# Low halves moved to VectorE and the exponents' clamp to GpSimd in the first block, one more unit scored in plain float32

## The chip, the cores and the metric

One NeuronCore of one Trainium2 chip. The metric is the device time of one execution in microseconds. Five engines run their own instruction queues in order: TensorE (PE, matrix products, with its weight loads shown as PEld), VectorE (DVE), ScalarE (ACT), GpSimd (POOL) and SyncE (SP), which issues all DMA transfers here. An engine waits for another through semaphores only.

## The reference

Three stages, in float32:

- Retention: for each of 4 x 8 heads a state of 64 x 64 decays by gamma at each of 768 positions and takes up the outer product of k and v; the output is q times the state. 
- A feed-forward layer on 3072 tokens: `h = x @ w_in` (512 to 2048), an ELU, `@ w_out` (2048 to 512).
- A second one: `h = x @ w_in` (512 to 1024), h times its softmax, a layer norm with gain `g_ln`, `@ w_out` (1024 to 512).

q, k and v come as float32; the weights of both layers are passed on as the bits of float64.

## The kernel before

Precision: a product of two float32 matrices is made of three passes in a rounded format, float32r. Each operand is split into a high half (the rounded copy) and a low half (the operand minus its high half); `mm3` multiplies high by high, high by low and low by high (L65 to L67).

Weights: a piece is [128, 512] in float64. `load_w` (L93) loads it, `abs_w` (L98, ScalarE) takes the absolute value of the upper word, `bits_w` (L103, VectorE) builds the float32 bits in four operations: clamp of the exponent (L107), first logical operation (L110), shift (L112), second logical operation (L114). A call works on two pieces, the first and third operation on one and the second and fourth on the piece before, alternating. `split_w` (L116) rounds the high half on ScalarE (L124) and subtracts the low half on GpSimd (L125). `prep_w` (L128) is one slot of this pipeline: split of piece n - 2, abs of n + 1, bits of n and n - 1, load of n + 3. Pieces stand in pools of four buffers.

Retention runs in chunks of 128 positions. A unit is a chunk's two head pairs. `att_scores_u` (L176) scores a whole unit in plain float32 and masks it on VectorE (L184); `att_scores` (L188) scores a pair from the split parts that `split_unit` (L165) makes on ScalarE and GpSimd (L170 to L173). Units below `UN` (17) go the first way. `att_values` (L205) makes the output of a pair (L225) and updates the state (L230, L233).

Order: the program is written out in the order of issue, without a scheduler. The start (L384 to L423) does eight units of retention and four slots of the weights' pipeline. The block loop (L426 to L507) has six blocks of 512 tokens with 16 steps each. A step s multiplies into the hidden layer (`ff1_in`), takes the ELU (`elu_a`, `elu_b`), handles one pair of retention for the block after, and multiplies out of the hidden layer for step s - 2 (`ff1_out`). In block 0 a step also holds two slots of `prep_w`. `elu_b` combines on VectorE (L276 in block 0), rounds the high half gh on ScalarE (L280), and subtracts the low half gl on GpSimd (L281). At a block's last step `split_xh` (L238, ScalarE) and `split_xl` (L244, VectorE) split the next block's input; it has one buffer. In the last block a step holds one slot of `prep_w` for the second layer's weights. A third loop (L511 to L526) does the second layer, 24 tiles of 128 tokens.

The functions and the lines that call them:

Of the kernel before, what the change touches and what calls it, by code (L numbers as in the profile page):

```python
# [9 lines left out]
F32 = mybir.dt.float32  # L10
F32R = mybir.dt.float32r
U32 = mybir.dt.uint32
AF = mybir.ActivationFunctionType
ALU = mybir.AluOpType
# [4 lines left out]
P = 128  # L19
B, H, S, D = 4, 8, 768, 64  # L20
NT = B * S
DM = H * D
FF1, FF2 = 2048, 1024
NP = H // 2          # head pairs; a pair fills 128 partitions
NCH = S // P         # chunks of a sequence
TB = 512             # tokens of a block of the first feed-forward layer
NB = NT // TB
CPB = TB // P
NF1 = FF1 // P
NF2 = FF2 // P  # L30
KD = DM // P
NU = B * NCH * 2      # a unit is a chunk's two head pairs
PPB = CPB * NP       # head pairs of a block
LAG = 2              # steps from a product into the hidden layer to the one out of it
HL = NF1 - 2         # step at which the weights are ready and the split of q and k begins
PRE = (2, 3, 4, 5)    # units of the start behind which a slot of the weights' pipeline lies
LEAD = 2             # pairs by which the attention is ahead of its block
UN = PPB + LEAD // 2  # units before this one score in plain float32
E_MIN, E_MAX = (float(x) for x in np.array([896 << 20, 1151 << 20], np.uint32).view(np.float32))
GAMMA = [1.0 - 2.0 ** (-5.0 - h) for h in range(H)]  # L40

# [2 lines left out]
def tile_retention_ffn(ctx, tc, k_t, qk_dup, qkv, w_in1, w_out1, w_in2, w_out2, g_ln, dmask, odec, kdec, ident_in, out):  # L44
    nc = tc.nc
# [4 lines left out]
    wa_p = ctx.enter_context(tc.tile_pool(name="wa", bufs=32))  # L50
# [10 lines left out]
    y_dr = [dram.tile([CPB, P, KD, P], F32, name=f"y_dr{i}") for i in range(NB)]  # L61

    def mm3(o, lh, ll, rh, rl, first, last):
        """o += (lh + ll).T @ (rh + rl) in float32r passes."""
        nc.tensor.matmul(o, lh, rh, start=first, stop=False)  # L65
        nc.tensor.matmul(o, lh, rl, start=False, stop=False)  # L66
        nc.tensor.matmul(o, ll, rh, start=False, stop=last)  # L67

    with tc.manual_schedule():
# [7 lines left out]
        wb_p = ph1.enter_context(tc.tile_pool(name="wb", bufs=32))  # L77
# [6 lines left out]
        stage_p = ph0.enter_context(tc.tile_pool(name="stage", bufs=4, side="right"))  # L84
        kblk = [at_p.tile([P, 2, 2, P], F32, name=f"kblk{i}", bufs=1) for i in range(2)]

# [1 line left out]
        # They come as float64, whose bits are cut to float32's here: a piece is [128, 512].  # L88
        raw_t, abs_t, w1i, w1o, w2i, w2o = {}, {}, {}, {}, {}, {}
        srcs = {"w1i": w_in1, "w1o": w_out1, "w2i": w_in2, "w2o": w_out2}  # L90
        dsts = {"w1i": w1i, "w1o": w1o, "w2i": w2i, "w2o": w2o}
# [3 lines left out]
            nc.sync.dma_start(out=t.rearrange("p a b -> p (a b)"), in_=srcs[x[0]][x[1]].bitcast(U32))  # L95
            raw_t[x] = t

        def abs_w(x):  # L98
            a = stage_p.tile([P, 512], U32, tag="wt", name="wt")
            nc.scalar.activation(a.bitcast(F32), raw_t[x][:, :, 1].bitcast(F32), AF.Abs)  # L100
            abs_t[x] = a

        def bits_w(x, y):  # L103
            """The first two operations on piece x and the last two on piece y."""
            if x:
                a = abs_t[x]
                nc.vector.tensor_scalar(a.bitcast(F32), a.bitcast(F32), E_MAX, E_MIN, ALU.min, ALU.max)  # L107
            if y:
                t, b = raw_t.pop(y), abs_t[y]
                nc.vector.scalar_tensor_tensor(b, t[:, :, 1], 0xC0000000, b, ALU.bitwise_and, ALU.bitwise_or)  # L110
            if x:
                nc.vector.tensor_scalar(a, a, 3, 0x3FFFFFF8, ALU.logical_shift_left, ALU.bitwise_and)  # L112
            if y:
                nc.vector.scalar_tensor_tensor(b, t[:, :, 0], 29, b, ALU.logical_shift_right, ALU.bitwise_or)  # L114

        def split_w(x):  # L116
            name, f = x
            w = abs_t.pop(x).bitcast(F32)
            if name == "w2o":
                nc.vector.tensor_scalar(w, w, g_sb[:, f:f + 1], None, ALU.mult)  # L120
            pool, tag = (wb_p, "wb") if name == "w1o" else (wa_p, "wa")
            hi = pool.tile([P, 512], F32R, tag=tag, name=f"{name}h")
            lo = pool.tile([P, 512], F32R, tag=tag, name=f"{name}l")
            nc.scalar.copy(hi, w)  # L124
            nc.gpsimd.tensor_tensor(lo, w, hi.bitcast(F32), ALU.subtract)  # L125
            dsts[name][f] = (hi, lo)

        def prep_w(order, n):  # L128
            """One slot of the weights' pipeline."""
            at = lambda i: order[i] if 0 <= i < len(order) else None  # L130
            if at(n - 2):
                split_w(at(n - 2))
            if at(n + 1):
                abs_w(at(n + 1))
            bits_w(at(n), at(n - 1))
            if at(n + 3):
                load_w(at(n + 3))

# [2 lines left out]
            order1 += [x for x in (("w1o", f), ("w1i", f + 3)) if x[1] < NF1]  # L141
        order2 = [("w2i", j) for j in range(2 * KD)] + [("w2o", j) for j in range(NF2)]

# [1 line left out]
        qk_t, in_t, hl_t, p_t = {}, {}, {}, {}  # L145

        def load_unit(u):
# [15 lines left out]
            nc.gpsimd.tensor_tensor(kt, kt, kd_sb[:, h:h + 4].unsqueeze(2).to_broadcast([P, 4, D]), ALU.mult)  # L163

        def split_unit(u):  # L165
            """q's and k's parts: q's high one twice over and its low one, k's high one over its low one."""
            t = qk_t.pop(u)
            q2 = hl_p.tile([P, 4, 2, P], F32R, tag="q2", name="q2")
            k2 = hl_p.tile([P, 4, P], F32R, tag="k2", name="k2")
            nc.scalar.copy(k2, t[:, 1])  # L170
            nc.scalar.copy(q2[:, :, 0, :], t[:, 0])
            nc.gpsimd.tensor_tensor(k2[D:], t[D:, 1], k2.bitcast(F32)[D:], ALU.subtract)
            nc.gpsimd.tensor_tensor(q2[:, :, 1, :], t[:, 0], q2.bitcast(F32)[:, :, 0, :], ALU.subtract)  # L173
            hl_t[u] = (q2, k2)

        def att_scores_u(u, bank):  # L176
            """A unit's scores in plain float32."""
            h = 4 * (u % 2)
            pt = at_p.tile([P, 4, P], F32, tag="pt", name="pt")
            sc = bank.rearrange("p (h t) -> p h t", h=4)  # L180
            for i in range(2):
                for j in range(2):
                    nc.tensor.matmul(sc[:, 2 * i + j, :], kblk[u % 2][:, i, j, :], in_t[u][:, i * P:(i + 1) * P], start=True, stop=True)
            nc.vector.tensor_tensor(pt, sc, dm_sb[:, h:h + 4, :], ALU.mult)  # L184
            for i in range(2):
                p_t[2 * u + i] = pt[:, 2 * i:2 * i + 2, :]

        def att_scores(n, bank):  # L188
            """A pair's scores from the split parts."""
            u, i = divmod(n, 2)  # L190
            h = 4 * (u % 2) + 2 * i
            pt = at_p.tile([P, 2, P], F32, tag="pt", name="pt")
            q2, k2 = hl_t[u]
            sc = bank.rearrange("p (j a t) -> p j a t", j=2, a=2)
            for j in range(2):
                nc.tensor.matmul(sc[:, j].rearrange("p a t -> p (a t)"), k2[:, 2 * i + j, :], q2[:, 2 * i + j].rearrange("p a t -> p (a t)"), start=True, stop=True)
            sa = hl_p.tile([P, 2, P], F32, tag="sa", name="sa")
            nc.scalar.copy(sa, sc[:, :, 1, :])  # L198
            nc.vector.tensor_tensor(pt, sa, sc[:, :, 0, :], ALU.add)  # L199
            nc.vector.tensor_tensor(pt, pt, dm_sb[:, h:h + 2, :], ALU.mult)  # L200
            if i:
                del hl_t[u]
            p_t[n] = pt
# [42 lines left out]
            for cc in cs:  # L246
                engines[cc % len(engines)].tensor_tensor(xl[:, cc], xf[:, cc], xh.bitcast(F32)[:, cc], ALU.subtract)  # L247

# [1 line left out]
        h_t, g_t, acc_t = {}, {}, {}  # L250

        def ff1_in(s):
# [18 lines left out]
        def elu_b(s, on_act):  # L271
            e = g_t[s]
            gh = g_p.tile([P, TB], F32R, tag="gh", name="gh")
            gl = g_p.tile([P, TB], F32R, tag="gl", name="gl")
            if on_act:
                nc.vector.scalar_tensor_tensor(e, e, -1.0, h_t.pop(s), ALU.add, ALU.max)  # L276
            else:
                nc.vector.tensor_scalar(e, e, 1.0, -1.0, ALU.min, ALU.add)  # L278
                nc.vector.tensor_tensor(e, e, h_t.pop(s), ALU.max)  # L279
            nc.scalar.copy(gh, e)  # L280
            nc.gpsimd.tensor_tensor(gl, e, gh.bitcast(F32), ALU.subtract)  # L281
            g_t[s] = (gh, gl)

        def new_acc(tb):
# [19 lines left out]
                    nc.sync.dma_start(out=y_dr[tb][:, :, m, :].rearrange("c p t -> p c t"), in_=yt.rearrange("p (c t) -> p c t", c=CPB))  # L304
                del acc_t[tb]

# [1 line left out]
        N2 = NT // P  # L308
        yin, ysp, h2, zc_t, rs_t, zt_t, op_t = {}, {}, {}, {}, {}, {}, {}

# [70 lines left out]
                nc.sync.dma_start(out=out[i * P:(i + 1) * P, :], in_=ot)  # L381
                del zt_t[i], op_t[i]

# [1 line left out]
        nc.vector.memset(state, 0.0)  # L385
        for kb in kblk:
            for j in range(2):
# [12 lines left out]
        load_unit(2)  # L400
        scale_k(0)
        slot = -1
        XLE = (nc.vector,)
        UB = PPB // 2
        for u in range(UB):
            if u + 1 < UB:
# [15 lines left out]
                prep_w(order1, slot)  # L422
                slot += 1  # L423

# [1 line left out]
        NS = NB * NF1  # L426
        NPR = B * NCH * NP
        for s in range(NS + LAG):
# [35 lines left out]
            if tb == 0:  # L464
                prep_w(order1, slot)
                slot += 1
            if s == HL:
                for i in range(slot, len(order1) + 2):
                    prep_w(order1, i)
# [67 lines left out]
def _layouts(q, k, v, moe_w_in, moe_w_out, moe2_w_in, moe2_w_out, moe2_g_ln):  # L537
# [10 lines left out]
    gam = 1.0 - 2.0 ** (-5.0 - h)  # L548
    t = np.arange(P)
    qp, kp, kr, vr = pairs_t(q), pairs_t(k), rows(k), rows(v)  # L550
    # a unit is two pairs: [unit, partition, ...]
    by_unit = lambda a: np.moveaxis(a.reshape(B * NCH, P, 2, NP // 2, P), 2, 1).reshape(NU, P, 2, P)
    by_unit_r = lambda a: np.moveaxis(a.reshape(B * NCH, P, 2, 4 * D), 2, 1).reshape(NU, P, 4 * D)
    heads_t = lambda a: by_unit(a).reshape(NU, 2, D, 2, P).transpose(0, 2, 3, 1, 4).reshape(NU, D, 4, P)
# [37 lines left out]
```

## Time and profile before

| what | value |
|---|---|
| timed runs | 975.77, 976.54, 977.78 us; median 976.54 |
| profiled execution, first to last instruction (span) | 976.4 us; the page gives no other time for it |
| TensorE busy | 941.1 us, 96% of the span |
| VectorE busy | 518.3 us, 53% |
| GpSimd busy | 393.3 us, 40% |
| ScalarE busy | 350.6 us, 36% |
| mean granted TensorE clock | 0.984 of full speed |
| DMA engines | 25% of their time, 85 GB/s |
| start, to about 38 us | eight units of retention |
| block 0, about 38 to 170 us | VectorE busy nearly throughout |
| blocks 1 to 4, about 180 to 600 us | TensorE busy throughout |
| block 5 with the second layer's weights, 600 to 705 us | TensorE and VectorE both busy |
| second layer, 705 to 976 us | TensorE busy |

Busy time counts an instruction from its start to its end, waits inside it included. The granted clock is the share of full speed that TensorE was given; its levels are 1.2 and 2.4 GHz. A matrix product's end is modelled, so TensorE's times are best read from start to start.

### The profile page before, as it was taken

How to read it: one execution, taken by the hardware profiler on the slowest of the kernel's cores; microseconds unless marked ns; L12 is line 12 of the kernel's file. 1: busy time of each engine (PE TensorE's matmuls, PEld its weight loads, DVE VectorE, ACT ScalarE, POOL GpSimd, SP SyncE). 2: the span in 40 equal slices, each digit the busy share in tenths (PEclk: the TensorE clock that was granted, in tenths of full speed). 3: DMA queues.
4: the chain of work that ended last, by engine and by line, in shares of the span. 5: the costliest groups of instructions: out<-in, count | busy, mean ns of one | idle time of the engine just before them, and what ended most of it. 6: DMA issues, size and time to landing. Idle time of an engine off the chain costs nothing.

```text
span 976.4 us, 12567 instructions
## 1 busy us (share of the span) xinstructions
PE 941.1 (96%) x4772; PEld 770.9 (79%) x4772; DVE 518.3 (53%) x962; ACT 350.6 (36%) x633; POOL 393.3 (40%) x359
## 2 busy tenths in 40 slices
PE   6888897999999999999999999999999999999998
PEld 5766675788878887878878887888888888888886
DVE  3899998443353435433353334999734433443332
ACT  1344445233333324333343333444333333333332
POOL 2255556444444344444444432466432222222221
PEclk9989999899999999999999999999999999999999
DMA  7545442322213222311232211521211111111101
GB/s 251 170 149 166 142 162 89 119 77 76 76 41 116 76 76 76 116 52 65 76 118 77 88 43 49 156 101 65 76 45 43 44 44 44 44 44 44 44 22 43
DMA packets 43691, 83.06 MB, mean 85 GB/s; under 512 B 4080, under 2 KB 20848, under 8 KB 43632
## 3 DMA queue, kind: packets, MB, share of 16 engines
q1 hardware_dynamic: 43632, 82.27, 25.3%
q8 instruction: 37, 0.61, 0.2%
q14 instruction: 22, 0.18, 0.1%
HBM read 69.67 MB, written 12.58 MB: 84 GB/s over the span
## 4 chain that ended last, share of the span: by engine, by line
PE 80%; DVE 13%; issue 3%; DMA 2%; ACT 0%; POOL 0%; SPq 0%; ACTq 0%; POOLq 0%
PE hp L66 12%; PE hp L65 12%; PE hp L67 12%; PE acc L65 8%; PE acc L66 7%; PE acc L67 7%; PE op L66 4%; PE op L65 4%; PE op L67 4%; DVE wt L114 3%; DVE wt L110 3%; PE yu_bank L216 2%; PE tp L365 2%; DVE wt L107 2%; DMA kblk<-in_k_t 1%
## 5 line engine op out<-in xcount | busy, mean ns | idle before, releaser
L281 POOL TENSOR_TENSOR gl<-e,gh 128x512 fp32r<-128x512 f32 x96 | 128.6, 1340 | 286.3 <-ACT gh L280 213.1
L65 PE MATMUL acc<-gh,w1oh 128*128 128x512 f32 x384 | 161.5, 421 | 0.0
L66 PE MATMUL acc<-gl,w1oh 128*128 128x512 f32 x384 | 153.8, 401 | 0.0
L67 PE MATMUL acc<-gh,w1ol 128*128 128x512 f32 x384 | 153.3, 399 | 0.0
L65 PE MATMUL hp<-xh,w1ih 128*128 128x512 f32 x384 | 152.1, 396 | 0.0
L66 PE MATMUL hp<-xl,w1ih 128*128 128x512 f32 x384 | 151.3, 394 | 0.4 <-DVE xl L247 0.4
L67 PE MATMUL hp<-xh,w1il 128*128 128x512 f32 x384 | 150.7, 392 | 0.4 <-POOL w1il L125 0.2
L280 ACT CAST gh<-e 128x512 fp32r<-128x512 f32 x96 | 59.6, 621 | 166.5 <-DVE e L279 123.5
L268 ACT ACTIVATE e<-hp 128x512 f32<-128x512 f32 x80 | 47.8, 598 | 148.9 <-PE hp L67 148.9
L65 PEld LDWEIGHTS acc<-gh,w1oh 128*128 128x128 f32 x384 | 74.0, 193 | 20.5 <-issue 2.4
L199 DVE TENSOR_TENSOR pt<-sa,sc_bank 128x256 f32<-128x256 f32 x62 | 26.1, 421 | 117.4 <-ACT sa L198 117.3
L67 PEld LDWEIGHTS acc<-gh,w1ol 128*128 128x128 f32 x384 | 74.3, 193 | 16.5
L67 PEld LDWEIGHTS hp<-xh,w1il 128*128 128x128 f32 x384 | 72.7, 189 | 16.8 <-POOL w1il L125 1.2
L66 PEld LDWEIGHTS acc<-gl,w1oh 128*128 128x128 f32 x384 | 74.2, 193 | 13.5
L66 PEld LDWEIGHTS hp<-xl,w1ih 128*128 128x128 f32 x384 | 73.0, 190 | 13.7 <-DVE xl L247 1.1
L65 PEld LDWEIGHTS hp<-xh,w1ih 128*128 128x128 f32 x384 | 73.1, 190 | 13.4
L278 DVE TENSOR_SCALAR e<-e 128x512 f32<-128x512 f32 x80 | 35.2, 440 | 79.3 <-ACT e L268 78.6
L65 PE MATMUL op<-w2oh,zh 128*128 128x512 f32 x192 | 76.7, 399 | 0.0
L66 PE MATMUL op<-w2ol,zh 128*128 128x512 f32 x192 | 74.8, 390 | 0.0
L67 PE MATMUL op<-w2oh,zl 128*128 128x512 f32 x192 | 74.8, 390 | 0.0
L67 PE MATMUL hp<-w2ih,yl 128*128 128x512 f32 x192 | 74.8, 389 | 0.0
L65 PE MATMUL hp<-w2ih,yh 128*128 128x512 f32 x192 | 74.8, 389 | 0.0
(99 smaller groups left out, 1617.6 us busy)
## 6 DMA issues: line engine op xcount, KB each, us to landing
in<-in_qkv SPq DMA_DIRECT2D x48, 384.0 KB, 4.1
qk<-in_qk_dup SPq DMA_DIRECT2D x31, 512.0 KB, 3.5
raw<-in_w_in SPq DMA_DIRECT2D x24, 512.0 KB, 3.6
raw<-in_w_out SPq DMA_DIRECT2D x24, 512.0 KB, 3.5
y_dr<-yt SPq DMA_DIRECT2D x24, 256.0 KB, 3.0
yin<-y_dr SPq DMA_DIRECT2D x24, 256.0 KB, 2.8
out<-ot SPq DMA_DIRECT2D x24, 256.0 KB, 2.0
kblk<-in_k_t SPq DMA_DIRECT2D x34, 64.0 KB, 4.3
```

The source lines that it names most:

```text
L65: nc.tensor.matmul(o, lh, rh, start=first, stop=False)
L66: nc.tensor.matmul(o, lh, rl, start=False, stop=False)
L67: nc.tensor.matmul(o, ll, rh, start=False, stop=last)
L107: nc.vector.tensor_scalar(a.bitcast(F32), a.bitcast(F32), E_MAX, E_MIN, ALU.min, ALU.max)
L110: nc.vector.scalar_tensor_tensor(b, t[:, :, 1], 0xC0000000, b, ALU.bitwise_and, ALU.bitwise_or)
L114: nc.vector.scalar_tensor_tensor(b, t[:, :, 0], 29, b, ALU.logical_shift_right, ALU.bitwise_or)
L199: nc.vector.tensor_tensor(pt, sa, sc[:, :, 0, :], ALU.add)
L216: nc.tensor.matmul(yu[j * D:(j + 1) * D, i, 0, :], v[:, j * D:(j + 1) * D], pt[:, j, :], start=(c == 0), stop=True)
L268: nc.scalar.activation(e, h_t[s], AF.Exp)
L278: nc.vector.tensor_scalar(e, e, 1.0, -1.0, ALU.min, ALU.add)
L280: nc.scalar.copy(gh, e)
L281: nc.gpsimd.tensor_tensor(gl, e, gh.bitcast(F32), ALU.subtract)
```

## The change

In the weights' pipeline the clamp moves to GpSimd, right behind abs; the other three bit operations of a piece follow each other on VectorE, all in one slot; the subtraction of the low half moves from GpSimd to VectorE. This holds for both layers' weights. In block 0, gl is subtracted on VectorE at the end of the step instead of on GpSimd; in the other blocks it stays on GpSimd. Of the four subtractions of the first block's xl, every second goes to GpSimd. `UN` becomes 18: one more unit is scored in plain float32, and the split of q and k begins with unit 18. Comments were dropped.

```diff
-UN = PPB + LEAD // 2  # units before this one score in plain float32
+UN = PPB + LEAD // 2 + 1
...
-        def abs_w(x):
+        def clamp_w(x):
             a = stage_p.tile([P, 512], U32, tag="wt", name="wt")
             nc.scalar.activation(a.bitcast(F32), raw_t[x][:, :, 1].bitcast(F32), AF.Abs)
+            nc.gpsimd.tensor_scalar(a.bitcast(F32), a.bitcast(F32), E_MAX, E_MIN, ALU.min, ALU.max)
             abs_t[x] = a
 
-        def bits_w(x, y):
-            """The first two operations on piece x and the last two on piece y."""
-            if x:
-                a = abs_t[x]
-                nc.vector.tensor_scalar(a.bitcast(F32), a.bitcast(F32), E_MAX, E_MIN, ALU.min, ALU.max)
-            if y:
-                t, b = raw_t.pop(y), abs_t[y]
-                nc.vector.scalar_tensor_tensor(b, t[:, :, 1], 0xC0000000, b, ALU.bitwise_and, ALU.bitwise_or)
-            if x:
-                nc.vector.tensor_scalar(a, a, 3, 0x3FFFFFF8, ALU.logical_shift_left, ALU.bitwise_and)
-            if y:
-                nc.vector.scalar_tensor_tensor(b, t[:, :, 0], 29, b, ALU.logical_shift_right, ALU.bitwise_or)
-
-        def split_w(x):
+        def bits_w(x):
+            t, b = raw_t.pop(x), abs_t[x]
+            nc.vector.tensor_scalar(b, b, 3, 0x3FFFFFF8, ALU.logical_shift_left, ALU.bitwise_and)
+            nc.vector.scalar_tensor_tensor(b, t[:, :, 1], 0xC0000000, b, ALU.bitwise_and, ALU.bitwise_or)
+            nc.vector.scalar_tensor_tensor(b, t[:, :, 0], 29, b, ALU.logical_shift_right, ALU.bitwise_or)
+
+        def high_w(x):
             name, f = x
-            w = abs_t.pop(x).bitcast(F32)
+            w = abs_t[x].bitcast(F32)
             if name == "w2o":
                 nc.vector.tensor_scalar(w, w, g_sb[:, f:f + 1], None, ALU.mult)
             pool, tag = (wb_p, "wb") if name == "w1o" else (wa_p, "wa")
             hi = pool.tile([P, 512], F32R, tag=tag, name=f"{name}h")
+            nc.scalar.copy(hi, w)
+            dsts[name][f] = hi
+
+        def low_w(x):
+            name, f = x
+            w, hi = abs_t.pop(x).bitcast(F32), dsts[name][f]
+            pool, tag = (wb_p, "wb") if name == "w1o" else (wa_p, "wa")
             lo = pool.tile([P, 512], F32R, tag=tag, name=f"{name}l")
-            nc.scalar.copy(hi, w)
-            nc.gpsimd.tensor_tensor(lo, w, hi.bitcast(F32), ALU.subtract)
+            nc.vector.tensor_tensor(lo, w, hi.bitcast(F32), ALU.subtract)
             dsts[name][f] = (hi, lo)
 
         def prep_w(order, n):
-            """One slot of the weights' pipeline."""
+
             at = lambda i: order[i] if 0 <= i < len(order) else None
             if at(n - 2):
-                split_w(at(n - 2))
+                high_w(at(n - 2))
             if at(n + 1):
-                abs_w(at(n + 1))
-            bits_w(at(n), at(n - 1))
+                clamp_w(at(n + 1))
+            if at(n):
+                bits_w(at(n))
+            if at(n - 2):
+                low_w(at(n - 2))
             if at(n + 3):
                 load_w(at(n + 3))
...
             nc.scalar.copy(gh, e)
-            nc.gpsimd.tensor_tensor(gl, e, gh.bitcast(F32), ALU.subtract)
+            g_t[s] = (e, gh)
+            if not on_act:
+                elu_c(s, nc.gpsimd)
+
+        def elu_c(s, engine):
+            e, gh = g_t[s]
+            gl = g_p.tile([P, TB], F32R, tag="gl", name="gl")
+            engine.tensor_tensor(gl, e, gh.bitcast(F32), ALU.subtract)
             g_t[s] = (gh, gl)
...
-        XLE = (nc.vector,)
+        XLE = (nc.vector, nc.gpsimd)
...
             if tb == 0:
                 prep_w(order1, slot)
                 slot += 1
+                elu_c(s, nc.vector)
             if s == HL:
```

## Rows read from the trace of the kernel before

**Rows 1.** The page's first part: busy us, share of the span, instructions.
```profile
PE 941.1 (96%) x4772; PEld 770.9 (79%) x4772; DVE 518.3 (53%) x962; ACT 350.6 (36%) x633; POOL 393.3 (40%) x359
```
**Rows 2.** Busy time by stretch: length, each engine's busy us (instructions), granted clock, DMA.
```profile
45.66:162.53 116.87, 102.73 (x501) 81.55 (x500) 116.49 (x158) 55.83 (x97) 66.85 (x49) 0.91 0.45 152
162.50:177.30 14.80, 10.38 (x42) 8.03 (x41) 9.46 (x16) 6.89 (x13) 10.08 (x7) 0.78 0.17 62
640.00:660.00 20.00, 20.00 (x90) 16.57 (x89) 19.45 (x22) 8.79 (x16) 12.72 (x9) 1.00 0.28 100
```
**Rows 3.** Groups by line, VectorE, 45.66 to 162.53: busy us, mean ns | idle before.
```profile
L225 DVE TENSOR_TENSOR xf<-yu_bank,od_sb 128x256 f32<-128x256 f32 x7 | 2.9, 410 | 0.0
L233 DVE SCALAR_TENSOR_TENSOR state<-state,yu_bank 64x64 f32<-64x64 f32 x12 | 2.1, 213 | 0.0
L230 DVE COPY state<-yu_bank 64x128 f32<-64x128 f32 x4 | 1.1, 282 | 0.0
```
**Rows 4.** Timeline of VectorE in block 0: start us, duration us, instruction.
```profile
113.48 1.52 DVE L112 TENSOR_SCALAR wt<-wt 128x512 uint32<-128x512 uint32 x1
...
118.93 0.68 DVE L110 SCALAR_TENSOR_TENSOR wt<-raw,wt 128x512 uint32<-128x512 uint32 x1
119.53 0.41 DVE L112 TENSOR_SCALAR wt<-wt 128x512 uint32<-128x512 uint32 x1
...
120.58 0.69 DVE L276 SCALAR_TENSOR_TENSOR e<-e,hp 128x512 f32<-128x512 f32 x1
121.18 0.68 DVE L184 TENSOR_TENSOR pt<-sc_bank,dm_sb 128x512 f32<-128x512 f32 x1
```
**Rows 5.** Timeline of GpSimd, start and block 0.
```profile
25.62 0.61 POOL L163 TENSOR_TENSOR in<-in,kd_sb 128x256 f32<-128x256 f32 x1 [3.36 <-PE acc L220]
...
113.40 1.31 POOL L281 TENSOR_TENSOR gl<-e,gh 128x512 fp32r<-128x512 f32 x1 [2.27 <-issue]
...
117.43 1.29 POOL L125 TENSOR_TENSOR w1ol<-wt,w1oh 128x512 fp32r<-128x512 f32 x1 [0.26 <-ACT w1oh L124]
```
**Rows 6.** Timeline of VectorE: xl at the start, two operations on one piece.
```profile
34.57 1.29 DVE L247 TENSOR_TENSOR xl<-xf,xh 128x512 fp32r<-128x512 f32 x2
...
163.13 0.68 DVE L110 SCALAR_TENSOR_TENSOR wt<-raw,wt 128x512 uint32<-128x512 uint32 x1
163.84 0.69 DVE L114 SCALAR_TENSOR_TENSOR wt<-raw,wt 128x512 uint32<-128x512 uint32 x1
```
**Rows 7.** Line L347 (second layer): duration ns min/median/max, first and last start.
```profile
L347 POOL TENSOR_SCALAR z<-z,st x23: 1122/1125/1133, 704.8 to 961.4; 128x1024 f32<-128x1024 f32 x23
```
**Rows 8.** Timeline of TensorE over two steps of block 0.
```profile
126.86 0.39 PE L65 MATMUL hp<-xh,w1ih 128*128 128x512 f32 x1
...
138.78 0.44 PE L216 MATMUL yu_bank<-pt,in 128*64 128x128 f32 x4 [1.52 <-DVE pt L184]
...
142.12 0.39 PE L65 MATMUL hp<-xh,w1ih 128*128 128x512 f32 x1
```
**Rows 9.** Timeline of VectorE, ScalarE and TensorE from block 0 to block 1.
```profile
162.53 0.68 DVE L276 SCALAR_TENSOR_TENSOR e<-e,hp 128x512 f32<-128x512 f32 x1
...
166.13 0.59 ACT L265 ACTIVATE e<-hp 128x512 f32<-128x512 f32 x1
...
167.29 2.16 ACT L242 CAST xh<-xf 128x512 fp32r<-128x512 f32 x4
...
171.57 0.80 PE L196 MATMUL sc_bank<-q,k 128*128 128x256 f32 x2 [4.42 <-POOL q L173]
172.17 0.63 PE L65 MATMUL hp<-xh,w1ih 128*128 128x512 f32 x1
...
177.29 0.50 PE L214 MATMUL yu_bank<-in,state 128*128 128x128 f32 x2
```
**Rows 10.** Timeline of TensorE at the start: products that wait for masked scores.
```profile
33.60 0.44 PE L216 MATMUL acc<-pt,in 128*64 128x128 f32 x4 [1.44 <-DVE pt L184]
```

More of the change, by code (lines that the diff above doesn't have):

```diff
@@ L273, in elu_b @@
             gh = g_p.tile([P, TB], F32R, tag="gh", name="gh")
-            gl = g_p.tile([P, TB], F32R, tag="gl", name="gl")
             if on_act:
```

## The prediction

> **What bounds the kernel now.** I read the page first: TensorE is busy for 96% of the span and VectorE for 53% [rows 1]. A mean over stages decides nothing here, so the next view is busy time by stretch [rows 2]. In the last block (640 to 660 us) TensorE has no idle time at all; what VectorE or GpSimd do there is hidden unless they fall behind. In the first block (45.66 to 162.53 us) it is the other way round: VectorE is busy for 116.49 of 116.87 us, and TensorE runs at a granted clock of 0.91. So in the first block VectorE sets the pace: 14 steps of the block loop, 8.35 us each. Behind it, 162.5 to 177.3 us, TensorE is busy for 10.4 of 14.8 us at a clock of 0.78: that is the passage from block 0 to block 1.
>
> Why does VectorE need 8.35 us? Its durations alone don't say. L112 takes 0.41 us at 119.53 but 1.52 us at 113.48 [rows 4]. That second one starts with GpSimd's subtraction of 113.40, which runs 1.31 us [rows 5], and it ends 0.29 us after it. So a VectorE instruction on SBUF waits while a GpSimd instruction runs, and the wait is counted as busy. Price both engines free of this. On VectorE I count from start to start: 0.60 us for L110 and L276 (each overlaps the next by 0.08), so about 0.34 for L112's 0.41 [rows 4]; L114 has L110's form, L107 that of L112, L184 the size of L276; the reads of the attention's sums take 2.9 + 2.1 + 1.1 = 6.1 us in the stretch [rows 3]. Per slot of the weights' pipeline 0.34 + 0.60 + 0.34 + 0.60 = 1.88 us. In 14 steps: 28 slots 52.6, 14 L276 8.4, 7 L184 4.2, and the 6.1: 71.3 us. The stretch takes 116.9, so 45.6 us are waits for GpSimd. GpSimd's own work, free, is 42 subtractions of 1.29 and 7 scalings of 0.61 us [rows 5]: 58.5 us. So 0.78 of GpSimd's time ends up as delay of VectorE; the rest falls beside instructions that read PSUM.
>
> **The change, part by part.**
>
> *Work of VectorE in the first block.* Per slot the clamp (0.34) goes; the low half's subtraction comes. Its form, two SBUF inputs and an fp32r output, is that of xl: two in 1.29 us [rows 6], so 0.60 from start to start (1.29 less one duration of 0.68). A second, less visible part: the three remaining operations of a piece now follow each other on one tile, where before two pieces alternated. The trace has one such pair: L110 at 163.13 and L114 at 163.84 work on the same piece [rows 6], 0.71 apart instead of 0.60, so a dependence costs 0.11 us. A piece has two of these: 0.45 + 0.71 + 0.60 = 1.76 us. A slot is then 1.76 + 0.60 = 2.36 us, 28 of them 66.1. Per step there is also gl's subtraction, 0.60: 14 make 8.4. With L276 8.4, L184 4.2 and 6.1: 93.2 us. VectorE alone gets 21.9 us more work.
>
> The Trainium skill speaks against my 0.11 us ("VectorE: DVE Perf Modes", section "The DRAIN you can't avoid": every operation drains the pipe anyway, and a semaphore behind each of eight copies cost nothing extra). By it the dependences are free and the sum comes out as in rival 5. The pair in rows 6 contradicts it, and I go by the row.
>
> *Work of GpSimd.* 42 subtractions go, 28 clamps come, 7 scalings stay. The trace has no clamp on GpSimd. The nearest row is L347, one tensor in, twice the elements, two operations: 1.125 us [rows 7]. Ends: 0.56 (half of it) and 1.29 (the subtraction with two inputs). I take 0.65, near the half, since what an instruction spends on its start isn't halved. 28 x 0.65 + 4.3 = 22.5 us instead of 58.5. At the same 0.78 this delays VectorE by 17.6 us. Sum 93.2 + 17.6 = 110.8 us, 6.1 less than 116.9. If all of it delayed VectorE: 115.7; if none did, TensorE would be next (below).
>
> The Trainium skill ("GPSIMD Engine Reference", section 3.1) puts a body of up to two operations at 1.03 cycles of 1.2 GHz per element: an estimate from it is 0.44 us for 512 elements, and the sum would be 960. No run here shows that price; the row at 1,024 elements is above what that rule gives (0.88 us).
>
> What is late next? TensorE needs, for two steps, 126.86 to 142.12 less one wait of 1.52: 13.7 us [rows 8], 96.2 for 14 steps. VectorE's 110.8 is still more; it stays the bound, at 7.9 us a step. ACT issues no more than before; its copies of the high halves no longer wait for bits done in the slot just before, and the clamp sits between ACT's abs and the bits of the next slot, half a step later. On the SP queue a piece's load needs only bits done a slot earlier, so loads behind it (kblk) go out sooner. None of this ends last.
>
> *Passage to block 1.* Here the extra plain float32 unit acts. TensorE waits 4.42 us for the low part of q (GpSimd, L173) and then begins block 1's first products at 172.17 at the lower of its two levels; they end at 177.29 [rows 9], 14.8 us after L276 of step 14 (162.53). Afterwards unit 17 needs no split; unit 18's is due two steps later, where TensorE has work in between. GpSimd's three last subtractions of block 0 are gone from its queue as well. From L276 of step 14 (0): it ends at 0.6, then ACT in order gh and two high halves (copies of an xh's size, 2.16 / 4 = 0.54 each), relu and exp (1.16 together, 166.13 to 167.29), up to 3.4; four xh 2.16 us [rows 9], to 5.6; VectorE's four xl follow 0.60 apart without GpSimd in their way, the first done near 4.8, the last near 6.6. TensorE meanwhile does the products that don't need block 1's x, until about 5.6, then 12 products at the higher level, 2.7 us (90 in 20.00 us [rows 2]): 8.3 instead of 14.8. Gain 6.5 us; 4.1 if the products still run at the lower level (177.29 - 172.17 = 5.1 us instead of 2.7).
>
> *Start.* Three slots' bits are on VectorE before block 0, with TensorE waiting 1.44 us for VectorE's pt [rows 10]. Before: 3 x 0.68 + 2 x 1.2 = 4.4 us; after: 3 x 1.76 + 0.6 = 5.9; plus 1.5. Two of four xl go to GpSimd: up to 1.2 back. Two clamps may delay VectorE by 0.65 each. Taken: 1.0 us later; bounds -0.5 and 2.8.
>
> *Last block.* Second-layer pieces get the same edit under a TensorE that never idles. VectorE: +0.60 - 0.34 + 0.22 = 0.48 us more per step; GpSimd's delay falls by 0.78 x (1.29 - 0.65) = 0.50. Equal: 0 us, hidden by TensorE's 24 products a step, 5.3 us at 90 in 20. If the cover were gone (VectorE is at 19.45 of 20 us [rows 2]), each 0.1 us over would cost 1.6 us over 16 steps.
>
> *Sum.* +1.0 - 6.1 - 6.5 = -11.6 us on a span of 976.4, which is 0.1 below the median of the timed runs (976.54): 964.9, said as 965.
>
> **Rivals.**
>
> 1. *VectorE no longer waits for GpSimd, TensorE becomes the bound.* If a clamp with one input doesn't hold up VectorE, 14 steps fall to TensorE's 96.2: -20.7, in all -26.2: 950. For: no row shows a one-input GpSimd instruction beside a VectorE one with two SBUF inputs. Against: a one-input VectorE instruction (L112) is held up by GpSimd.
> 2. *Every clamp delays VectorE in full.* 115.7 us: -1.2 in the block, -6.7 in all: 970; 972 if the passage keeps the lower level. For: more of VectorE's instructions now read SBUF alone, so fewer PSUM ones cover GpSimd.
> 3. *The passage gives nothing.* Block 1 waits for xl where it waited for q. +1.0 - 6.1: 971. For: x has one buffer, so xh can't start before the last step's products. Against: the layout above.
> 4. *Slower: the clamp costs what a two-input instruction does.* Place: the 28 slots of block 0. At 1.29 us GpSimd has 40.4 us, 31.5 of it delay: 124.7, +7.8, in all +2.3: 979; 988 if all of it delays. It decides from 1.18 us a clamp, where 93.2 + 0.78 x (28 x 1.18 + 4.3) eats the passage's gain. For: min and max on GpSimd stand in no row. Against: L347 does two operations on 1,024 elements in less than that.
> 5. *The dependences between a piece's operations cost nothing.* 28 x 0.22 = 6.2 us less: 959. For: the 0.11 us rest on one pair. Against: that pair.
>
> **How the numbers follow.** Forecast 48%, its own range 960 to 969; rival 1 14%, rival 2 19%, rival 3 7%, rival 4 7%, rival 5 5%. What can be told from no change is 0.2%, 2 us. All but rival 4 are faster by more: 93%, of which I put 3% near zero where rivals 2 and 3 meet. Faster 0.90, same 0.04, slower 0.06. The range runs from between rival 1 and the forecast's lower end (952) to past rivals 2 and 3 (973); outside are rival 4 and about half of rival 1, some 14%.
>
> **What would show it.** In the trace of the changed kernel: L276 to L276 in block 0 at 7.9 us (6.9 for rival 1, 8.3 for rival 2, 8.9 for rival 4); a clamp alone on GpSimd at 0.65 us; shift and first logical operation 0.45 apart; a VectorE subtraction 0.60 when GpSimd is idle; no wait of TensorE for q's low part near block 1's start, and its first products without a stretch at the lower level; TensorE still without idle time in the last block. The prediction is wrong if the 14 steps take under 100 or over 118 us, or if the passage still takes more than 11 us from step 14's L276.

## The result, and the profile after

The changed kernel takes 962.34 us (median; 959.46 to 963.23). The kernel before, run beside it, takes 976.95 (975.77 to 977.78). The ratio is 0.9845 [0.9829, 0.9861]: 14.6 us less, where the prediction had 11.6.

The page's first part for the changed kernel, columns as in [rows 1]: the changed kernel has a span of 957.4 us, GpSimd's busy time falls from 393.3 to 343.4 us, and VectorE's falls too although it was given more instructions.

```profile
PE 928.2 (97%) x4776; PEld 761.4 (80%) x4776; DVE 499.8 (52%) x973; ACT 347.7 (36%) x629; POOL 343.4 (36%) x343
```

Busy time by stretch of the changed kernel, columns as in [rows 2]. The first row is the 14 steps of block 0 (step 0's L278, which was L276, to that of step 14), the second the passage to block 1, exactly from step 14's L278 to the first product behind block 1's first products (yu_bank from state, 157.46). The third answers to the last row of [rows 2].

```profile
45.30:149.66 104.36, 94.43 (x507) 76.69 (x508) 102.06 (x172) 55.15 (x97) 30.77 (x35) 1.00 0.54 171
149.66:157.46 7.80, 7.70 (x43) 5.91 (x41) 6.55 (x16) 5.38 (x10) 0.00 (x0) 1.00 0.00 0
640.00:660.00 20.00, 20.00 (x89) 16.54 (x89) 19.62 (x29) 8.74 (x16) 10.89 (x9) 1.00 0.19 54
```

The 14 steps took 116.87 us and take 104.36: 7.45 a step instead of 8.35. The passage took 14.76 (162.53 to 177.29, [rows 9]) and takes 7.80, with no work on GpSimd in it and TensorE busy for 7.70 of it. In both stretches the granted clock is now 1.00, where it was 0.91 and 0.78. VectorE is still busy for 102.06 of 104.36 us in the steps and TensorE for 94.43: VectorE remains the bound. The higher clock isn't what shortened the steps: in e6 below they ran at 0.97 and took 116.87 us as before. In the last block TensorE still has no idle time.

All experiments are divided in the same way, each from its own profiled execution (us):

| kernel | span | start, to step 0's L278 | 14 steps | passage | the rest |
|---|---|---|---|---|---|
| before | 976.4 | 45.66 | 116.87 | 14.76 | 799.1 |
| changed | 957.4 | 45.30 | 104.36 | 7.80 | 799.9 |
| e1: unit 17 split again | 961.6 | 45.51 | 104.97 | 10.93 | 800.2 |
| e2: two pieces in turn | 950.5 | 44.19 | 98.50 | 7.80 | 800.0 |
| e3: clamp in halves | 958.5 | 47.18 | 103.56 | 7.81 | 800.0 |
| e4: gl on GpSimd | 966.3 | 48.69 | 108.19 | 9.46 | 800.0 |
| e5: changed, once more | 960.7 | 48.54 | 104.37 | 7.81 | 800.0 |
| e6: before, unit 17 unsplit | 972.8 | 46.27 | 116.87 | 10.51 | 799.2 |
| e7: clamp on VectorE | 964.7 | 45.89 | 110.28 | 7.80 | 800.7 |
| e8: all xl on VectorE | 956.4 | 44.25 | 104.35 | 7.80 | 800.0 |

By spans the change is worth -0.4 - 12.5 - 7.0 + 0.8 = -19.0 (from unrounded stages). The medians differ by 14.6. Steps, passage and rest repeat to 0.1 us when the same kernel is profiled again (e5); the start doesn't, and the changed kernel's profiled execution was the shortest of its four. So the other 4.4 us lie in the start, as far as the traces can tell.

Where VectorE's time went is read from groups by line, VectorE, in the 14 steps (busy us, mean ns of one | idle before). First the kernel before:

```profile
L112 DVE TENSOR_SCALAR wt<-wt 128x512 uint32<-128x512 uint32 x28 | 36.8, 1313 | 0.0
L114 DVE SCALAR_TENSOR_TENSOR wt<-raw,wt 128x512 uint32<-128x512 uint32 x29 | 27.3, 942 | 0.0
L110 DVE SCALAR_TENSOR_TENSOR wt<-raw,wt 128x512 uint32<-128x512 uint32 x28 | 26.7, 953 | 0.0
L107 DVE TENSOR_SCALAR wt<-wt 128x512 f32<-128x512 f32 x28 | 16.5, 589 | 0.2
```

The same view of the changed kernel:

```profile
L107 DVE SCALAR_TENSOR_TENSOR wt<-raw,wt 128x512 uint32<-128x512 uint32 x28 | 22.1, 790 | 1.0
L108 DVE SCALAR_TENSOR_TENSOR wt<-raw,wt 128x512 uint32<-128x512 uint32 x28 | 19.4, 692 | 1.0
L125 DVE TENSOR_TENSOR w1il<-wt,w1ih 128x512 fp32r<-128x512 f32 x15 | 13.2, 878 | 0.0
L290 DVE TENSOR_TENSOR gl<-e,gh 128x512 fp32r<-128x512 f32 x14 | 12.9, 919 | 0.0
L106 DVE TENSOR_SCALAR wt<-wt 128x512 uint32<-128x512 uint32 x28 | 12.7, 454 | 0.2
```

What a mean has above the undisturbed duration is waiting for GpSimd. This wait lies inside an instruction that has begun, with no semaphore: that engines wait through semaphores only, as the first section has it, is too narrow. Undisturbed, a one-input operation takes 0.41 us and the others 0.68 before; in the changed kernel it is 0.418 for the shift, 0.692 for the logical operations (as L108 here) and 0.684 for the subtractions (as L125 in e7). Before: 28 x (1.313 - 0.41) + 29 x (0.942 - 0.68) + 28 x (0.953 - 0.68) + 28 x (0.589 - 0.41) = 45.5 us. After: L107 28 x (0.790 - 0.692) + L125 15 x (0.878 - 0.684) + L290 14 x (0.919 - 0.684) + L106 28 x (0.454 - 0.418) = 10.0 us (the expectations say 11.2; with 0.41 and 0.68 throughout it is 11.0). The waits fall by 35.5 and the steps by 12.5, so by this difference VectorE's own work rose by about 23 us. The prediction had 21.9 for the work, and 17.6 us of waits left.

### The profile page after: what moved, and what is told of

It reads as the page before. It is cut to its first block, busy times and chain, and to the rows that moved or that the text cites. A ratio compares the mean times of both kernels' runs of the same rounds, so it can differ in the third digit from the quotient of the medians.

```text
span 957.4 us, 12608 instructions
## 1 busy us (share of the span) xinstructions
PE 928.2 (97%) x4776; PEld 761.4 (80%) x4776; DVE 499.8 (52%) x973; ACT 347.7 (36%) x629; POOL 343.4 (36%) x343
## 4 chain that ended last, share of the span: by engine, by line
PE 79%; DVE 14%; DMA 2%; issue 2%; ACT 1%; POOL 0%; SPq 0%; ACTq 0%; DVEq 0%
PE hp L66 11%; PE hp L65 11%; PE hp L67 11%; PE acc L65 9%; PE acc L66 7%; PE acc L67 7%; PE op L66 5%; PE op L65 5%; PE op L67 5%; DVE wt L107 2%; PE yu_bank L219 2%; PE tp L374 2%; DVE xl L250 2%; PE sc_bank L199 1%; DVE wt L106 1%
## 5 line engine op out<-in xcount | busy, mean ns | idle before, releaser
L290 POOL TENSOR_TENSOR gl<-e,gh 128x512 fp32r<-128x512 f32 x80 | 108.6, 1357 | 255.9 <-ACT gh L282 203.5
L65 PE MATMUL acc<-gh,w1oh 128*128 128x512 f32 x384 | 158.1, 412 | 0.0
L66 PE MATMUL acc<-gl,w1oh 128*128 128x512 f32 x384 | 150.2, 391 | 0.0
L67 PE MATMUL acc<-gh,w1ol 128*128 128x512 f32 x384 | 150.0, 391 | 0.0
L65 PEld LDWEIGHTS acc<-gh,w1oh 128*128 128x128 f32 x384 | 72.0, 187 | 19.6 <-issue 2.7
L67 PEld LDWEIGHTS acc<-gh,w1ol 128*128 128x128 f32 x384 | 72.1, 188 | 15.8
L66 PEld LDWEIGHTS hp<-xl,w1ih 128*128 128x128 f32 x384 | 72.4, 189 | 14.7 <-DVE xl L250 1.7
L66 PEld LDWEIGHTS acc<-gl,w1oh 128*128 128x128 f32 x384 | 72.2, 188 | 12.7
```

What stands on the lines that cost most here:

```text
L290: engine.tensor_tensor(gl, e, gh.bitcast(F32), ALU.subtract)
```

## The experiments

**e1. The extra plain float32 unit taken back.** The changed kernel with one line altered:

```
-UN = PPB + LEAD // 2 + 1
+UN = PPB + LEAD // 2
```

> The changed kernel with unit 17 scored from the split parts again, all else as changed. In its trace the passage from step 14's L278 of block 0 to the end of block 1's first products took 7.8 us, 14.8 before the change. Theory A (the plain float32 unit gives the passage): TensorE waits again for q's low part, the passage goes back to 13 to 15 us, 6 to 7 us slower than the changed kernel, near 969. Theory B (GpSimd's queue, now without three subtractions, gives it): q's split ends early enough, the passage takes 9 to 10.5 us, 1.5 to 3 us slower, near 964.

Measured: 964.35 us, ratio to before 0.9871 [0.9845, 0.9897]; passage 10.93. Busy time by stretch of e1's passage:

```profile
150.48:161.41 10.93, 9.01 (x39) 6.57 (x38) 9.64 (x18) 6.68 (x13) 3.92 (x3) 0.87 0.23 84
```

TensorE's only wait in it, from the view of waits of e1 (total us, times, longest):

```profile
PE sc_bank L199 <- POOL q L176: 1.9, 1, 1.9
```

The wait for q's low part is back, but it is 1.9 us instead of 4.42: GpSimd has three operations in the stretch and not seven ([rows 2], second row), and the three subtractions that stood in front of q's split are gone. So the rest of the changes takes 14.76 - 10.93 = 3.8 us from the passage without the extra unit. That the unit alone carries the passage (theory A) is out; 10.93 lies above theory B's range too, so GpSimd's queue doesn't carry it alone either. Part of what a wait for q costs is the clock behind it: 0.87 here and 0.78 before, 1.00 in e6 and in the changed kernel.

**e6. The extra unit alone, in the kernel before.**

```
-UN = PPB + LEAD // 2
+UN = PPB + LEAD // 2 + 1
```

> The kernel before with unit 17 scored in plain float32, nothing else. The passage took 14.8 us before; with all of the change 7.8; with all but this part about 11. If the two parts add up, this one alone gives 3.4 us: passage 11 to 11.5, total near 973. If the waits stand behind each other (q's split also holds up ScalarE's relu and xh), it gives 5 to 6 us: passage 9 to 10, near 971. Theory A of the first run (it gives the whole): 7.8, near 969.5.

Measured: 973.34 us, 0.9955 [0.9941, 0.997]; the 14 steps unchanged, passage 10.51. Busy time by stretch of e6's passage:

```profile
163.14:173.65 10.51, 7.74 (x34) 5.19 (x32) 8.59 (x15) 5.51 (x11) 6.87 (x5) 1.00 0.00 0
```

TensorE's longest wait in it, from the view of waits of e6:

```profile
PE hp L66 <- DVE xl L247: 2.1, 2, 1.4
```

Without the wait for q, TensorE waits for xl, on a VectorE that GpSimd's 6.87 us of remaining work hold up. The unit alone gives 4.25 us, the rest alone 3.8, both 7.0. The two causes add up but for 1.1 us (10.51 lies between the ranges of the first two cases); the passage belongs to neither of them.

**e2. Two pieces in turn on VectorE.** Two pieces alternate again, as before the change, with the three operations that VectorE has left; all else as changed:

```
+        def bits_w(x, y):
+            if x:
+                a = abs_t[x]
+                nc.vector.tensor_scalar(a, a, 3, 0x3FFFFFF8, ALU.logical_shift_left, ALU.bitwise_and)
+            if y:
+                t, b = raw_t.pop(y), abs_t[y]
+                nc.vector.scalar_tensor_tensor(b, t[:, :, 0], 29, b, ALU.logical_shift_right, ALU.bitwise_or)
+            if x:
+                nc.vector.scalar_tensor_tensor(a, raw_t[x][:, :, 1], 0xC0000000, a, ALU.bitwise_and, ALU.bitwise_or)
...
-            if at(n):
-                bits_w(at(n))
+            bits_w(at(n), at(n - 1))
```

> The changed kernel with the bit operations of two pieces alternating: shift of piece n, last operation of piece n - 1, first logical operation of n, then the low half of n - 2, so that no operation follows one that it depends on. If a dependence costs 0.11 to 0.12 us as the traces' starts show (0.45 and 0.73 instead of 0.34 and 0.60), block 0's 14 steps fall from 104.4 to about 98 us, 6 us faster than the changed kernel, near 956; TensorE's 96.2 us are then close. Rival (the gap is filled by GpSimd's waiting instructions anyway, or dependences cost nothing): within 2 us of the changed kernel.

Measured: 953.82 us, 0.9773 [0.9753, 0.9792]; 14 steps 98.50. Timeline of VectorE in the changed kernel, then in e2 (start us, duration us, instruction):

```profile
113.38 0.42 DVE L106 TENSOR_SCALAR wt<-wt 128x512 uint32<-128x512 uint32 x1
113.83 0.69 DVE L107 SCALAR_TENSOR_TENSOR wt<-raw,wt 128x512 uint32<-128x512 uint32 x1
114.56 0.69 DVE L108 SCALAR_TENSOR_TENSOR wt<-raw,wt 128x512 uint32<-128x512 uint32 x1
115.17 1.10 DVE L125 TENSOR_TENSOR w1il<-wt,w1ih 128x512 fp32r<-128x512 f32 x1
```

```profile
100.54 0.41 DVE L107 TENSOR_SCALAR wt<-wt 128x512 uint32<-128x512 uint32 x1
100.88 0.68 DVE L110 SCALAR_TENSOR_TENSOR wt<-raw,wt 128x512 uint32<-128x512 uint32 x1
101.48 0.68 DVE L112 SCALAR_TENSOR_TENSOR wt<-raw,wt 128x512 uint32<-128x512 uint32 x1
102.08 0.68 DVE L129 TENSOR_TENSOR w1il<-wt,w1ih 128x512 fp32r<-128x512 f32 x1
```

On one piece the starts lie 0.45 and 0.73 us apart, on two pieces 0.34 and 0.60. That is 0.24 us a slot or 6.7 over 28; the steps lose 5.9, since the waits for GpSimd, taken from e2's groups as above, rise from 10.0 to 10.7. So the dependences cost what the prediction charged, and rival 5 is out. This version is the shortest of all that were run. Its 7.04 us a step stand close to the 6.85 that the prediction read for TensorE from [rows 8].

**e3. The clamp in two column halves.** This asks how much of a GpSimd instruction holds VectorE up.

```
-            nc.gpsimd.tensor_scalar(a.bitcast(F32), a.bitcast(F32), E_MAX, E_MIN, ALU.min, ALU.max)
+            for c in range(2):
+                nc.gpsimd.tensor_scalar(a.bitcast(F32)[:, c * 256:(c + 1) * 256], a.bitcast(F32)[:, c * 256:(c + 1) * 256], E_MAX, E_MIN, ALU.min, ALU.max)
```

> The changed kernel with each clamp on GpSimd as two instructions of 256 elements. In the changed kernel's trace a clamp takes 0.61 us alone, and a VectorE instruction that it holds up is 0.42 us longer (1.10 instead of 0.68); before, a subtraction of 1.30 us held up by 1.10. Theory A (the first 0.19 us of a GpSimd instruction don't hold up VectorE, the rest does): two halves hold up 0.42 together, block 0's 14 steps stay at 104 to 106 us, though GpSimd works 5 us longer. Theory B (a fixed share of GpSimd's time delays VectorE, 0.52 in the changed kernel, 0.78 before): 28 x 0.19 = 5.3 us more on GpSimd, 3 to 4 us more in the 14 steps. Theory C (each GpSimd instruction that is met costs a fixed hand-over): 28 more meetings, 5 us or more.

Measured: 957.76 us, 0.9814 [0.9793, 0.9834]; 14 steps 103.56, with GpSimd busy for 42.70 us in them instead of 30.77. Timeline of VectorE in e3 beside the two half clamps that run from 116.27 to 117.83:

```profile
116.68 0.88 DVE L126 TENSOR_TENSOR w1il<-wt,w1ih 128x512 fp32r<-128x512 f32 x1
117.49 0.88 DVE L291 TENSOR_TENSOR gl<-e,gh 128x512 fp32r<-128x512 f32 x1
...
118.74 0.77 DVE L108 SCALAR_TENSOR_TENSOR wt<-raw,wt 128x512 uint32<-128x512 uint32 x1
```

The half clamps of e3 in the whole trace (duration ns min/median/max, first and last start):

```profile
L102 POOL TENSOR_SCALAR wt<-wt x96: 399/833/843, 16.5 to 663.2; 128x256 f32<-128x256 f32 x96
```

Each half holds one subtraction up by 0.88 - 0.68 = 0.20 us. A whole clamp holds it up by 1.10 - 0.68 = 0.42 (115.17 in the changed kernel), a subtraction of before by 1.52 - 0.41 = 1.11 [rows 4]. Undisturbed, a half clamp takes 0.40 us (the shortest of the 96; beside VectorE's work they too become longer), a clamp 0.61 (below), a subtraction 1.29 to 1.31 [rows 5]. The difference is 0.20, 0.19 and 0.18 to 0.20 us: a VectorE operation right behind an independent one is held up for GpSimd's undisturbed duration less a fixed 0.2 us. Hold-ups in proportion to GpSimd's time (theory B) or a fixed cost for each meeting (theory C) would have made the steps longer; they became 0.8 us shorter, a little below theory A's 104 to 106. Of the waits for GpSimd some 7.7 us are left, and VectorE waits once for TensorE, 1.2 us. The kernel's median is 4.6 us below the changed kernel's, more than its steps explain; its profiled execution was the longest of its four (960.36), and the rest lies in the start, as far as the traces can tell.

The fixed 0.2 us isn't shown to be the first part of GpSimd's instruction. The lines shown say when a held-up operation ends: L125 0.55 us after the clamp (116.27 for 115.72, below), L291 0.54 after the two halves (118.37 for 117.83), the one-input L112 0.29 after the subtraction of before (115.00 for 114.71). The timelines of the 14 steps of before, changed, e2, e3, e4 and e7 have some 200 such meetings, and in all of them it is 0.28 to 0.29 us with one input and 0.54 to 0.55 with two. So the hold-up lasts until GpSimd's instruction ends, and only some 0.13 us of VectorE's own operation (0.41 - 0.28, 0.68 - 0.55) run beside it. An operation that depends on the one in front starts 0.12 us later and is held up by that much less: 0.08 us for L108 of 118.74 above.

The clamp's own duration, from GpSimd's timeline of the changed kernel: once with VectorE out of its way, and once in block 0, where it begins beside L108 of 114.56 and is itself 0.42 us longer.

```profile
16.67 0.61 POOL L101 TENSOR_SCALAR wt<-wt 128x512 f32<-128x512 f32 x1 [1.74 <-ACT wt L100]
...
114.69 1.03 POOL L101 TENSOR_SCALAR wt<-wt 128x512 f32<-128x512 f32 x1 [4.88 <-ACT wt L100]
```

**e4. gl back on GpSimd.** Fourteen long subtractions return to GpSimd and leave VectorE.

```
-            if not on_act:
-                elu_c(s, nc.gpsimd)
+            elu_c(s, nc.gpsimd)
...
-                elu_c(s, nc.vector)
```

> The changed kernel with block 0's gl subtracted on GpSimd again, right behind gh. VectorE loses 14 x 0.60 = 8.4 us, GpSimd gains 14 x 1.29 = 18 us. By hold-ups of 1.10 us each where met (the changed kernel's 35 short GpSimd instructions cost 11.2 of a possible 14.7 us): 0.76 to 1 of 15.4 us, so the 14 steps take 104.4 - 8.4 + 12 to 15 = 108 to 111 us and the kernel is 3 to 7 us slower than the changed one. Rival (the stalls fall beside instructions that read PSUM): no slower.

Measured: 967.32 us, 0.9901 [0.9877, 0.9925]; 14 steps 108.19, as expected. VectorE has 14 x 0.60 = 8.4 us less work, and the steps are 3.8 us longer. Groups by line of e4, the four groups in which waits stand (L108, L107, L125 and L106 had 692, 790, 878 and 454 ns in the changed kernel):

```profile
L108 DVE SCALAR_TENSOR_TENSOR wt<-raw,wt 128x512 uint32<-128x512 uint32 x28 | 29.6, 1057 | 1.0
L107 DVE SCALAR_TENSOR_TENSOR wt<-raw,wt 128x512 uint32<-128x512 uint32 x28 | 26.5, 946 | 1.0
L125 DVE TENSOR_TENSOR w1il<-wt,w1ih 128x512 fp32r<-128x512 f32 x15 | 13.8, 918 | 0.0
L106 DVE TENSOR_SCALAR wt<-wt 128x512 uint32<-128x512 uint32 x28 | 13.1, 467 | 0.2
```

Reckoned as above, the waits are 22.2 us instead of 10.0: 12.2 more, less 8.4 of work, is the 3.8. A subtraction costs VectorE 0.60 us when VectorE does it and on average 0.87 us of waits when GpSimd does it; the operations that the subtractions meet here mostly depend on the one in front and are held up by 0.98 us, not 1.10. The rival is out. The passage grows to 9.46 us.

**e7. The clamp on VectorE.**

```
-            nc.gpsimd.tensor_scalar(a.bitcast(F32), a.bitcast(F32), E_MAX, E_MIN, ALU.min, ALU.max)
...
+            nc.vector.tensor_scalar(b.bitcast(F32), b.bitcast(F32), E_MAX, E_MIN, ALU.min, ALU.max)
             nc.vector.tensor_scalar(b, b, 3, 0x3FFFFFF8, ALU.logical_shift_left, ALU.bitwise_and)
```

> The changed kernel with the clamp as a fourth operation of a piece on VectorE instead of GpSimd. VectorE gains 28 x 0.45 = 12.6 us in block 0's 14 steps (0.34 and one dependence more), GpSimd keeps only the 7 scalings there: of 11.2 us of hold-ups 9 to 10 go. 14 steps: 104.4 + 12.6 - 9.5 = 107 to 108 us, 3 to 4 us slower than the changed kernel, near 966. Rival (my prediction's price for the clamp, 0.78 x 0.65 = 0.51 us each): 12.6 - 14.2, no slower, near 961.

Measured: 966.87 us, 0.9899 [0.9879, 0.9919]; 14 steps 110.28, 2 to 3 us above the expectation. The timeline of VectorE in e7 gives the price of the clamp there:

```profile
102.02 0.42 DVE L105 TENSOR_SCALAR wt<-wt 128x512 f32<-128x512 f32 x1
102.47 0.43 DVE L106 TENSOR_SCALAR wt<-wt 128x512 uint32<-128x512 uint32 x1
```

It is 0.45 us and not 0.34, since the shift waits for it: 28 x 0.45 = 12.6 us more work. What remains of the waits for GpSimd, from the groups by line of e7:

```profile
L107 DVE SCALAR_TENSOR_TENSOR wt<-raw,wt 128x512 uint32<-128x512 uint32 x28 | 20.0, 713 | 1.0
...
L106 DVE TENSOR_SCALAR wt<-wt 128x512 uint32<-128x512 uint32 x28 | 13.4, 480 | 1.0
```

28 x (0.713 - 0.692) + 28 x (0.480 - 0.418) = 2.3 us, by the seven scalings that GpSimd keeps. So the waits fall from 10.0 to 2.3 and the work grows by 12.6: 4.9 of the 5.9 us that the steps grew by. Another 0.9 us is one wait of VectorE for TensorE (view of waits of e7: L228 for yu_bank), which the changed kernel doesn't have. The rival, that the clamp on VectorE would be no slower, is out.

**e8 and e5. The start.** e8 puts all four xl before block 0 back on VectorE; e5 is the changed kernel without an edit.

```
-        XLE = (nc.vector, nc.gpsimd)
+        XLE = (nc.vector,)
```

> The changed kernel with all four low halves of the first block's input on VectorE. In the changed kernel one VectorE xl took 1.13 us (0.69 free), held up by GpSimd's xl, and TensorE waited 0.2 us for the last one. On VectorE 0.6 to 1.2 us more before step 0, less the 0.44 of the hold-up: 0 to 1 us slower, not to be told from the changed kernel. Rival (GpSimd's 1.3 us for an xl ends later than VectorE's would): up to 1 us faster.

> The changed kernel once more, on the chip and beside the runs of the next three. Its profiled execution was the shortest of its runs (span 957.4, granted clock 1.00; the others 960.4 to 961.2 at 0.994 to 0.996). If the 3 us between them lie in block 0, this trace shows a stretch at the lower level behind one of TensorE's waits for pt (1.8 us in the first trace) and a step longer by 1 us or more; if in the start, step 0's L278 comes later than 45.3 us.

Measured: e8 962.94 us, 0.9847 [0.9817, 0.9877]; e5 961.05 us, 0.9829 [0.9803, 0.9856]. The two can't be told apart, so the runs show no effect of the xl's engine at the start. e5's span is 3.3 us above that of the changed kernel's first trace, and all but 0.1 of it lies ahead of block 0. The stretch 20 to 40 us, first trace and then e5:

```profile
20.00:40.00 20.00, 16.65 (x156) 13.42 (x155) 16.59 (x44) 5.02 (x9) 7.73 (x10) 1.00 0.85 262
```

```profile
20.00:40.00 20.00, 16.30 (x122) 13.91 (x122) 15.05 (x40) 4.13 (x7) 5.61 (x8) 0.74 0.76 231
```

One kernel, two executions: 156 products at a granted clock of 1.00, 122 at 0.74, while the DMA engines moved 262 and 231 GB/s. Timeline of TensorE, first trace and then e5:

```profile
22.91 1.13 PE L186 MATMUL acc<-in,kblk 128*128 128x128 f32 x8 [1.08 <-DMA kblk<-in_k_t]
```

```profile
21.24 0.46 PE L186 MATMUL acc<-in,kblk 128*128 128x128 f32 x2 [0.75 <-DMA kblk<-in_k_t]
22.76 1.65 PE L186 MATMUL acc<-in,kblk 128*128 128x128 f32 x6 [1.06 <-DMA kblk<-in_k_t]
```

In e5 TensorE waits twice for keys from the DMA, with 0.46 us of products between the waits; the granted clock is 1.00 up to 22.0 us and 0.50 from 22.5 to 29. In the first trace there is one such wait in that stretch, and the clock stays at 1.00. So here products that come late stand in front of the lower clock; why the keys came later, and how much of the 3.3 us each of the two is worth, isn't shown.

## Why the prediction was right or wrong

*Right.* VectorE sets the pace of block 0 before and after, its waits for GpSimd are what the change removes, and the passage shrinks. The clamp took 0.61 us alone (0.65 predicted), shift and first logical operation are 0.45 apart (0.45), the undisturbed subtraction is 0.60, q's low part is waited for no longer, the passage runs at a granted clock of 1.00, and TensorE has no idle time between 640 and 660 us. VectorE's own work grew by about 23 us (21.9). On the price of a dependence e2 decides for the row: 0.45 and 0.73 us with, 0.34 and 0.60 without. The prediction had read the Trainium skill ("VectorE: DVE Perf Modes", section "The DRAIN you can't avoid") against it; that section's eight copies price a semaphore behind each operation, and it doesn't say that one copy needed the result of another.

*The failed step: "At the same 0.78 this delays VectorE by 17.6 us."* It was 10.0, 7.6 less and more than the whole miss in the 14 steps (104.36 for 110.8); VectorE's own work was about 1.1 more. The 0.78 was measured on instructions of 1.29 us and used on instructions of 0.65. By e3 an instruction holds up an independent VectorE operation for its duration less some 0.2 us. That is 1.10 of 1.30 us (0.85), but 0.42 of 0.61 (0.69). So the prediction's remark that the rest of GpSimd's time falls beside instructions that read PSUM is wrong for the larger part: of these 13 us the fixed part is 49 x 0.19 = 9.3. At these prices GpSimd could delay VectorE by 42 x 1.10 + 7 x 0.42 = 49.1 us before, of which 45.5 came about, and by 35 x 0.42 = 14.7 after, of which 10.0 did: the share that came about fell as well, from 0.93 to 0.68. The timelines say why. GpSimd and then VectorE in the changed kernel:

```profile
72.54 0.62 POOL L101 TENSOR_SCALAR wt<-wt 128x512 f32<-128x512 f32 x1 [1.33 <-ACT wt L100]
...
78.46 1.05 POOL L166 TENSOR_TENSOR in<-in,kd_sb 128x256 f32<-128x256 f32 x1
```

```profile
72.72 0.98 DVE L107 SCALAR_TENSOR_TENSOR wt<-raw,wt 128x512 uint32<-128x512 uint32 x1
...
78.96 0.41 DVE L228 TENSOR_TENSOR xf<-yu_bank,od_sb 128x256 f32<-128x256 f32 x1
```

Of the 35 GpSimd instructions 15 hold a subtraction up by 0.42 us; 9 meet the first logical operation, which depends on the shift, and hold it up by 0.29 to 0.38 (L107 at 72.72); 4 hold a shift up by 0.14 to 0.29; and 7, all scalings, run beside the read of an attention sum from PSUM, which loses nothing (L228 at 78.96). That makes 6.2 + 2.8 + 0.9 = 9.9 of the 10.0 us. The seven scalings met the same reads before, but there they were 2.9 of a possible 49.1 us and here 2.9 of 14.7.

Rival 1, that a one-input instruction holds nothing up, is out by the 1.10 us subtraction; rival 2 is out by the sum, rival 3 by the passage's 7.80, and rival 4 by the clamp's 0.61 us.

*The passage*, 7.80 for 8.3: right in size, partly by luck. TensorE began block 1's products 4.45 us after L278 and not at about 5.6, and the 12 products took 3.35 us and not 2.7. Its cause was put first on the extra unit and, in one sentence, on GpSimd's emptied queue. e1 and e6 show two nearly equal halves. The wait for q was the last of several; behind it lay waits for xl, which e6 makes visible.

*The start*, +1.0 predicted: the trace has -0.4, but the medians leave +4.1 (14.6 = 12.5 + 7.0 - 0.8 - 4.1), and with e5's 961.05 against the 977.79 of the kernel before beside it +1.9. Both are above the +1.0, with the spread between executions as large as the term. Why the start should be later in the median stays open; e8, no faster, gives no sign that it is the xl. It is luck that the whole came within 3 us: the steps gave 6.4 us more than forecast, and the start, by the medians, took 3.1 back.

*The rest*, 0 predicted, +0.8 measured, and not in the steps but at the end of block 5. Timeline of VectorE in the changed kernel there:

```profile
680.84 0.69 DVE L125 TENSOR_TENSOR w2ol<-wt,w2oh 128x512 fp32r<-128x512 f32 x1 [2.33 <-ACT w2oh L117]
681.45 1.22 DVE L350 TENSOR_REDUCE st<-hp 128x1 f32<-128x1024 f32 x1
```

The low half of a last second-layer piece waits 2.33 us on VectorE for ScalarE's high half, and the maximum of the next tile (L350) is queued behind it. On GpSimd the same wait held nothing of VectorE's. TensorE then waits 1.15 us for zl at 688.05 (0.31 before). From the maximum's start to zl's it is 5.78 us here and 5.79 before, so the delay is passed on whole; that the queued subtraction causes it was not tried by itself.

*The base.* The prediction took the profiled span (976.4) for 0.1 us below the median. In every run with both numbers the time is 1.8 to 2.1 us more than the span (here 959.46 for 957.4), so the profiled execution of before was some 1.8 us above its median. A difference of spans then has this error in it; the one of medians doesn't.

## What to carry to other kernels

Price the hold-up of one engine by another per instruction (here its duration less 0.2 us, 0.3 behind a dependence, times the instructions that meet work on SBUF alone), not as a share of its time: shorter instructions held up by a smaller share. When work moves onto a busy in-order engine, keep two independent tiles alternating on it, since here each dependence between neighbours cost 0.11 to 0.13 us and undoing them gave a further 5.9 us. When several waits end together, undo each edit alone and apply each alone before giving the gain to one of them.

## What was not expected of the hardware

A VectorE operation that GpSimd holds up ends a fixed time after GpSimd's instruction (0.28 to 0.29 us with one input, 0.54 to 0.55 with two), so the hold-up is GpSimd's duration less 0.18 to 0.20 us, at three durations (0.40, 0.61 and 1.30 us). The waiting goes both ways: the clamp of 114.69 takes 1.03 us beside VectorE instead of 0.61. And the granted clock of the same kernel over the same 20 us of its start was 1.00 in one execution and 0.74 in another, whose start was 3.2 us longer.
